# A range check of kept softmax sums, with a general version behind a branch, in a convolution and two-matmul kernel

## The chip, the cores and the metric

The kernel runs on one core of a Trainium2 chip. A core has five engines with instruction streams of their own: TensorE (PE in the profile; PEld is its weight load), VectorE (DVE), ScalarE (ACT), GpSimd (POOL) and SyncE (SP), which here only issues DMA transfers. They meet through semaphores. The metric is device time in microseconds of one execution.

## The reference

```python
def _attn_ref(x, weight_gen):            # x: 8 x 4096 x 192, weight_gen: 8 x 4096 x 8 x 7
    w = weight_gen - np.max(weight_gen, axis=-1, keepdims=True)
    w = np.exp(w)
    w = w / (np.sum(w, axis=-1, keepdims=True) + 1e-09)
    ...                                  # x_unf: the 7 last tokens of x, by head
    out = np.einsum('bshk,bskhg->bshg', w, x_unf)

def _moe_ref(x, w_in, w_out):            # w_in: 192 x 2048, w_out: 2048 x 192
    h = x @ w_in
    g = h - np.tanh(h)
    return g @ w_out
```

Each token has, for each of 8 heads, 7 weights from a softmax. They weigh the token and the 6 before it (a convolution with its own weights at each token). The result, 192 wide, goes through a matmul to 2048, `h - tanh(h)`, and a matmul back to 192. `weight_gen` is drawn from a normal distribution times 0.3, all in float32.

## The kernel before, in words

The 32,768 tokens are cut into 32 blocks of 1024 (`n`, `NTOT` = 32), and a block lies on 128 partitions with 8 tokens each (`J` = 8).

For each block, SP loads `x` and `weight_gen`. ACT takes the exponential without subtracting a maximum (`softmax_exp`). DVE sums over the 7 weights (`softmax_sum`, 64 sums per partition, in a tile `zsum` of which three buffers go round), takes the reciprocal and scales (`softmax_norm`). POOL makes most of the products of weights and tokens, with DMA transfers that add (`dma_sum`), and PE adds what is left while it transposes (`conv_sums`).

The first matmul of block `n` is cut into 16 tiles `f`. Per tile PE fills `ph`, ACT takes the tanh, and DVE subtracts into `gt` (`gemm1`). `ph` comes from three PSUM buffers. Between them PE works at the second matmul of the block before (`out_stream`), whose results ACT copies out (`store_out`), and SP stores a block when its eighth token group is done. A softmax is worked on four blocks ahead of its use: in the loop over `n`, `soft` names that block, and from `n` = 28 on there is none. Where a block has one, DVE does the reciprocal and the scaling between the subtractions of `f` = 14 and `f` = 15.

The order on each engine is written by hand: the whole body stands under `tc.manual_schedule()`, so an engine's instructions come in the order in which the Python code issues them, and semaphores are placed by what each reads and writes.

After the loop, the second matmul of the last block has nothing to lie beside. `gemm2_last(j)` does it by token group `j` (the j-th token of every partition, "token j" for short): 32 matmuls into a bank `po`, a copy of one half by ACT (`ot`), an add by DVE into `out_sb`, and after each second group a store of two of the eight groups on SP. Then the program's end waits for every transfer and the engines meet in a barrier.

Of the kernel before, what the change touches and what calls it, by code (L numbers as in the profile page):

```python
# [8 lines left out]
FP32 = mybir.dt.float32  # L9
BF16 = mybir.dt.bfloat16  # L10

ACT = mybir.ActivationFunctionType
AX = mybir.AxisListType


@with_exitstack
def kernel(
# [20 lines left out]
    JH = J // 2  # L38
    HT = TOK // 2
    NSB = S // TOK  # L40
    NTOT = B * NSB
    NFT = F // P
    NC = D // R
# [7 lines left out]
    HELP = {n: ((n - 2, 3),) for n in (4, 5, 6, 7, 8, 9, 10, 11, 12, 13, 14, 15, 16, 17, 18, 19, 20, 21, 22, 23, 24, 25, 26, 27, 28, 29, 30, 31)} | {9: ((7, 3), (6, 12)), 10: ((8, 3), (7, 12)), 11: ((9, 3), (8, 12)), 12: ((10, 3), (9, 12)), 13: ((11, 3), (10, 12)), 14: ((12, 3), (11, 12))}  # L51
    LAST_TAP = (4, 5, 6, 7, 8)
    X_LATE = ()
    ZERO_AT = 8
    PACE, PACED = None, ()
    SCALE_TWICE = True
# [24 lines left out]
    zero = const.tile([1, D], FP32, name="zero")  # L81
    nc.vector.memzero(zero[:])
    once = const.tile([P, 1], FP32, name="once")

    x_of = {}
    held = {}
# [2 lines left out]
    zsum_of = {}  # L89
    zr_of = {}  # L90
    wsm_of = {}
    prods_of = {}
    to_sum = {}
    conv_of = {}
# [72 lines left out]
    def softmax_exp(n):  # L167
        wg_t = wg_of.pop(n)
        last_exp[0] = nc.scalar.activation(  # L169
            out=wg_t[:].rearrange("p j h k -> p (j h k)"),  # L170
            in_=wg_t[:].rearrange("p j h k -> p (j h k)"),
            func=ACT.Exp,
        )
        e_of[n] = wg_t
# [4 lines left out]
    def softmax_sum(n, j0=0, j1=J):  # L179

        if j0 == 0:
            zsum_of[n] = wgpool.tile([P, J * H], FP32, name="zsum")
        nc.vector.reduce_sum(  # L183
            out=zsum_of[n][:, j0 * H : j1 * H],
            in_=e_of[n][:, j0:j1].rearrange("p j h k -> p (j h) k"),
            axis=AX.X,
        )

    def softmax_recip(n, j0=0, j1=J):
        if j0 == 0:  # L190
# [3 lines left out]
    def softmax_norm(n, bank):  # L194

        wsm = softmax_tile()
        zr_v = bank[:, 512 - J * H : 512]
        nc.vector.reciprocal(zr_v, zsum_of[n][:])  # L198

        def finish():  # L200
            scale(nc.vector, wsm[:], e_of[n], zr_v)

        wsm_of[n] = (wsm, None, None, None)
        return finish

    def softmax_norm_ramp(n, bank):

        softmax_sum(n)
        wsm = softmax_tile()
        zr_v = bank[:, 512 - J * H : 512]  # L210
        nc.vector.reciprocal(zr_v, zsum_of[n][:])  # L211
# [14 lines left out]
        wsm_of[n] = (wsm, wsm_v, None, None)  # L226
# [298 lines left out]
    def out_pairs(m):  # L525
        for _ in range(m):
            next(pairs)

    def gemm2_last(j, f0=0, f1=NFT):

        n = NTOT - 1
        if f0 == 0:
            half[j] = psum_h.tile([P, 2, HT], FP32, name="po2", tag="ph")
        po = half[j]
        col = (j % 2) * HT + (j // 2) * P
        for f in range(f0, f1):
            for r in range(2):
                nc.tensor.matmul(  # L538
                    po[:, r, 0:D],
                    lhsT=g_of[n][f][r * R : (r + 1) * R, col : col + P],  # L540
                    rhs=w_out[r * R : (r + 1) * R, f, :],
                    start=(f == 0),
                    stop=(f == NFT - 1),
                )
# [6 lines left out]
        nc.scalar.activation(out=ot[:], in_=po[:, 0, 0:D], func=ACT.Copy)  # L551
        nc.vector.tensor_add(out_sb[:, j, :], po[:, 1, 0:D], ot[:])
        if j % 2 == 1:
            nc.sync.dma_start(
                out=out[n * TOK : (n + 1) * TOK, :].rearrange("(p j) e -> p j e", p=P)[
                    :, j - 1 : j + 1, :
                ],
                in_=out_sb[:, j - 1 : j + 1, :],
            )

    w_in = const.tile([P, NC, F], BF16, name="w_in")
    w_out = const.tile([P, NFT, D], BF16, name="w_out")

    ctx.enter_context(tc.manual_schedule())

    def load_w_out():
        nc.gpsimd.dma_start(out=w_out[:], in_=moe_w_out.rearrange("(c p) e -> p c e", c=NFT))
# [139 lines left out]
    for n in range(1, NTOT):  # L707
        more = n < NTOT - 1
        finish = []
        plan = FIRST if n == 1 else DOUBLE if n in DOUBLE_IN else APART if n in APART_IN else STEADY  # L710

        soft = [m for m in (n + 3 if n <= AHEAD else n + 4,) if m < NTOT]
        for f in range(NFT):
            ph = gemm1(n, f)
            if n == 1:
                if f == 1:
                    load_wg(5)
                if f == 5:
                    softmax_exp(4)
                steps = ((softmax_sum, 3), (softmax_recip, 3), (softmax_sum, 4))  # L720
                for at, (step, m, h) in zip(plan["sums"], [s + (h,) for s in steps for h in (0, 1)]):
                    if f == at:
                        step(m, h * JH, (h + 1) * JH)
                if f == 5:
                    wsm_of[3] = (softmax_tile(), None, e_of[3], zr_of[3])
                    rest = products(3)
            elif f == 1:
                if soft:
                    softmax_exp(soft[0])
                if n + 2 < NTOT:  # L730
                    rest = products(n + 2)
            if n == AHEAD and f == 4:
                softmax_exp(n + 4)
            if n > 1:
                for h, at in enumerate(plan["sums"]):
                    if soft and f == at:
                        softmax_sum(soft[0], h * JH, (h + 1) * JH)
            if n == AHEAD:
                for at, (step, h) in zip(EXTRA, [(s, h) for s in (softmax_sum, softmax_recip) for h in (0, 1)]):
                    if f == at:  # L740
                        step(n + 4, h * JH, (h + 1) * JH)
                if f == EXTRA[-1]:
                    wsm_of[n + 4] = (softmax_tile(), None, e_of[n + 4], zr_of[n + 4])
            for m in (n + 2, n + 3):
                if (n, f) in HELP.get(m, ()):
                    help(m, ph, J - 1 - HELP[m].index((n, f)))
            if n + 2 < NTOT and f == (9 if n == 1 else max([b for a, b in HELP.get(n + 2, ()) if a == n] + [3])):
                rest()
            if f == (9 if n == 1 else 1) and n > STORE_FIRST:
                loads(n)  # L750
            done = 0
            for chunks, at in sorted((((0, 1), plan["t2"]), ((2,), plan["t1"])), key=lambda c: c[1]):
                if more and at[0] == f:
                    out_pairs(at[1] - done)
# [12 lines left out]
            if f == (9 if n == 1 else 1) and n <= STORE_FIRST:  # L767
                loads(n)

    gemm2_last(0, 0, J)  # L770
    out_pairs(NFT)
    gemm2_last(0, J, NFT)
    for j in range(1, J):
        gemm2_last(j)


# [28 lines left out]
```

## Time and profile before

| | |
|---|---|
| three runs | 745.0, 746.48 (median), 747.21 us |
| span of the profiled execution, first to last instruction | 743.4 us |
| its own device time | not listed; the runs lie 1.6 to 3.8 us above this span |
| mean granted TensorE clock | 0.995 |
| PE / DVE / ACT / POOL busy | 97% / 92% / 86% / 88% of the span |
| last matmul, last add on DVE, last store issued, end of the wait for it | 739.6, 740.3, 740.4, 742.2 us |

The profile is of one execution on the chip. Its page has the busy times of each engine, the span in 40 slices, the DMA queues, the chain of work that ended last, the costliest groups of instructions, and the DMA issues. Groups are named by line of the kernel, engine and operation, "out<-in", with shapes, count, busy time, mean time of one, and what ended the idle time before them. From the trace, questions can be asked of one stretch: busy times in windows, a timeline of an engine, the chain of waits in order of time, or one line's instructions. Matmuls are pipelined, so that a busy PE is not a PE at its peak. SPq is SP's queue: an issue's time there is that of issuing, not of the transfer.

### The profile page before, as it was taken

The numbers are of one execution on the slowest core, as the hardware profiler recorded it, in microseconds if no ns is written. First come the engines' busy times: TensorE is split into PE (matmuls) and PEld (weight loads), VectorE is DVE, ScalarE is ACT, GpSimd is POOL, SyncE is SP. The second block draws the span as 40 slices with busy tenths as digits, with TensorE's granted clock in tenths as the row PEclk, the third lists the DMA queues.
The fourth block names the chain that finished last, engine by engine and source line by source line (L and its number), as shares of the span: only waits on it lengthen the run. The fifth ranks groups of instructions, "written<-read, shape, count | busy, mean of one in ns | idle before, by whom it ended". The sixth has DMA issues, their size and how long they took to land.

```text
span 743.4 us, 30037 instructions
## 1 busy us (share of the span) xinstructions
PE 722.3 (97%) x13616; PEld 556.5 (75%) x13616; DVE 687.4 (92%) x723; ACT 638.8 (86%) x872; POOL 654.5 (88%) x163
## 2 busy tenths in 40 slices
PE   3899999999999999999999999999999999999997
PEld 2477777778777777777777777777777777877777
DVE  7999899999999999999999999999999999988893
ACT  4888888888888888989889999898998989888882
POOL 7999999999999999999999999999999999991000
PEclk9899999999999999999999999999999999999999
DMA  8925367766567668878777977877887877776112
GB/s 236 245 46 161 135 172 185 195 179 149 124 183 184 183 185 224 210 199 203 166 202 209 236 186 204 178 195 205 221 209 195 192 181 194 193 149 110 45 45 86
DMA packets 34269, 130.06 MB, mean 175 GB/s; under 512 B 4591, under 2 KB 9439, under 8 KB 30174
## 3 DMA queue, kind: packets, MB, share of 16 engines
q0 software_dynamic: 19424, 51.12, 40.4%
q1 hardware_dynamic: 14718, 77.03, 27.6%
q8 instruction: 106, 1.74, 0.9%
q14 instruction: 21, 0.17, 0.1%
HBM read 54.52 MB, written 25.17 MB: 107 GB/s over the span
## 4 chain that ended last, share of the span: by engine, by line
PE 92%; DVE 5%; ACT 1%; issue 1%; DMA 1%; SPq 0%; DVEq 0%
PE ph L427 43%; PE obank L495 43%; PE pc L384 4%; DVE gt L441 3%; PE po L538 1%; ACT th L440 1%; DVE pa L299 1%; DMA wg_t<-in_weight_gen_dram 1%; DVE zsum L183 0%; SPq L134 0%; ACT convT L402 0%; DVE obank L211 0%; DVE pa L251 0%; DVE pb L299 0%; SPq L144 0%
## 5 line engine op out<-in xcount | busy, mean ns | idle before, releaser
L441 DVE TENSOR_TENSOR gt<-ph,th 128x1024 bf16<-128x1024 f32 x512 | 601.6, 1217 | 33.4 <-ACT th L440 23.2
L440 ACT ACTIVATE th<-ph 128x1024 f32<-128x1024 f32 x512 | 512.1, 1025 | 69.2 <-PE ph L427 60.3
L427 PE MATMUL ph<-convT,w_in 64*128 64x512 bf16 x3072 | 415.1, 379 | 5.3 <-DVE gt L441 3.3
L495 PEld LDWEIGHTS <-gt 64*128 64x128 bf16 x7936 | 355.6, 94 | 80.6 <-issue 6.3
L495 PE MATMUL obank<-w_out,gt 64*128 64x192 bf16 x7936 | 408.0, 243 | 0.9 <-issue 0.8
L299 POOL TENSOR_TENSOR pa<-x_t,wsm 128x2688 bf16<-128x2688 f32 (+3 forms) x68 | 338.9, 5232 | 0.2
L299 POOL TENSOR_TENSOR pb<-x_t,wsm 128x4608 bf16<-128x4608 f32 (+2 forms) x33 | 283.8, 8601 | 0.7 <-ACT wsm L221 0.5
L427 PEld LDWEIGHTS <-w_in 64*128 64x128 bf16 x3072 | 163.0, 94 | 86.0 <-issue 18.3
L514 ACT ACTIVATE out_sb<-obank 128x192 f32<-128x192 f32 x248 | 81.3, 328 | 11.2 <-PE obank L495 10.3
L410 ACT ACTIVATE convT<-pc 128x1024 bf16<-128x1024 f32 (+1 forms) x62 | 50.1, 810 | 2.9 <-PE pc L384 2.7
L236 POOL DMA_DIRECT2D pa<-pb x28 | 36.0, 1284 | 13.7 <-POOL pb L299 9.1
L384 PEld LDWEIGHTS <-pa 64*128 64x128 bf16 x2064 | 41.5, 100 | 6.8 <-DVE pa L299 1.1
L236 POOL DMA_DIRECT2D pa<-pa x21 | 34.7, 1651 | 9.6 <-DMA pa<-pb 8.9
L384 PE MATMUL pc<-ident,pa 64*128 64x64 bf16 x1968 | 41.2, 191 | 1.8 <-POOL pa L299 0.9
L183 DVE TENSOR_REDUCE zsum<-wg_t 128x32 f32<-128x224 f32 (+1 forms) x61 | 23.6, 387 | 2.9 <-ACT wg_t L169 2.9
L169 ACT ACTIVATE wg_t<-wg_t 128x448 f32<-128x448 f32 x32 | 18.2, 570 | 6.3 <-DMA wg_t<-in_weight_gen_dram 6.2
L251 DVE TENSOR_TENSOR pa<-x_t,ph 128x384 bf16<-128x384 f32 x34 | 18.8, 554 | 2.0 <-DVE ph L250 0.3
L229 DVE TENSOR_TENSOR wsm<-wg_t,pc 128x448 f32<-128x448 f32 x27 | 16.8, 621 | 2.5
L198 DVE RECIPROCAL pc<-zsum 128x64 f32<-128x64 f32 x27 | 14.9, 550 | 0.0
L384 PE MATMUL pc<-ident,pb 64*128 64x64 bf16 x216 | 4.9, 206 | 9.0 <-POOL pb L299 9.0
L384 PEld LDWEIGHTS <-pb 64*128 64x128 bf16 x288 | 6.3, 106 | 9.5 <-POOL pb L299 9.0
L538 PE MATMUL po<-w_out,gt 64*128 64x192 bf16 x256 | 11.2, 243 | 0.0
(27 smaller groups left out, 56.8 us busy)
## 6 DMA issues: line engine op xcount, KB each, us to landing
x_t<-in_x_dram SPq DMA_DIRECT2D x31, 1344.0 KB, 7.9
pa<-pb POOLq DMA_DIRECT2D x28, 1152.0 KB, 9.5
out_dram<-out_sb SPq DMA_DIRECT2D x31, 768.0 KB, 3.9
pa<-pa POOLq DMA_DIRECT2D x21, 768.0 KB, 7.2
wg_t<-in_weight_gen_dram SPq DMA_DIRECT2D x32, 224.0 KB, 7.1
x_t<-in_x_dram SPq DMA_DIRECT2D x1, 768.0 KB
w_out<-in_moe_w_out_dram POOLq DMA_DIRECT2D x1, 768.0 KB, 9.5
out_dram<-out_sb SPq DMA_DIRECT2D x4, 192.0 KB, 3.0
```

What stands on the lines that cost most here:

```text
L183: nc.vector.reduce_sum(out=zsum_of[n][:, j0 * H : j1 * H], in_=e_of[n][:, j0:j1].rearrange("p j h k -> p (j h) k"), axis=AX.X,)
L236: return nc.gpsimd.dma_start(out=out.rearrange("p k j d -> p k (j d)"), in_=in_.rearrange("p k j d -> p k (j d)"), accum_op=mybir.AluOpTyp ...
L251: nc.vector.tensor_mul(pa[:, 0:KH, j, :].rearrange("p k (h g) -> p k h g", h=H), bass.AP(tensor=x_v.tensor, offset=x_v.offset + j * D, ap= ...
L299: return eng.tensor_mul(prod(k0, k1)[:, :, j0:j1].rearrange("p k j (h g) -> p k (j h) g", h=H), bass.AP(tensor=x_v.tensor, offset=x_v.offs ...
L384: nc.tensor.matmul(pc[r][:, col : col + R] if home else pc[:, r, col : col + R], lhsT=prods[c][gi][r * R : (r + 1) * R, 2 * j : 2 * j + 2] ...
L410: last_conv[0] = nc.scalar.activation(out=out, in_=pc[:, :, 0:cols].rearrange("p r (cj t) -> p r cj t", t=R), func=ACT.Copy,)
L427: nc.tensor.matmul(ph[:, r, :], lhsT=w_in[r * R : (r + 1) * R, c, f * P : (f + 1) * P], rhs=convT[r * R : (r + 1) * R, c, :], start=(c == ...
L440: last_act[0] = nc.scalar.activation(out=th[:], in_=ph_f, func=ACT.Tanh)
L441: last_sub[0] = nc.vector.tensor_sub(gt[:], ph_f, th[:])
L495: mm = nc.tensor.matmul(po[:, 0:D], lhsT=g_of[n][f][r * R : (r + 1) * R, col : col + P], rhs=w_out[r * R : (r + 1) * R, f, :], start=(r == ...
L514: last_act[0] = nc.scalar.activation(out=out_sb[:, j, :], in_=po[:, 0:D], func=ACT.Copy)
L538: nc.tensor.matmul(po[:, r, 0:D], lhsT=g_of[n][f][r * R : (r + 1) * R, col : col + P], rhs=w_out[r * R : (r + 1) * R, f, :], start=(f == 0 ...
```

## The change

The kernel leaves the maximum out of its softmax, which is exact as long as the sums stay within the range of float32. The change adds a look at this, and a second version of the whole computation for the case that they don't.

- All sums are kept in one tile, `zall` (128 x 2048, float32), of which block `n` has 64 columns. The three buffers `zsum` go.
- `sums_piece` has eight pieces. 0 to 3 are reductions of 128 x 1024 sums to one column: the maxima of the two halves, then the minima. 4 and 5 compare (`<= 1e30`, `>= 1e-18`), 6 multiplies the answers to two columns and sends them with a DMA on SP to one row of 256, and 7 takes the minimum of that row to an integer, `flag`. Pieces 0, 1 and 2 stand behind tile `f` = 14 of blocks 28, 29 and 30, pieces 3 to 6 behind the last tile of block 31, and 7 ahead of token group 4 of the last block.
- The last block's stores are cut anew: groups 0 and 1, groups 2 and 3, group 4 alone, and groups 5 to 7 together.
- The manual schedule ends, every engine loads `flag` into a register, and a conditional block stands ahead of the last store. If the flag is 0, `general` goes over all 32 blocks again with the maximum subtracted, in loops that run on the chip. If it is 1, which it is for these inputs, nothing of this runs.

In the built program the order on PE, ACT and POOL is as before up to the register load. DVE gets the reductions and comparisons where they are written. SP gets the flag's DMA ahead of the store of block 30, then the stores of groups 0 to 1 and 2 to 3, the register load with a range check of the value, the store of group 4, and the conditional branch. On the way that runs here, SP next waits on each of the eight semaphores of its transfers, so for all that it has issued, jumps over the instructions of the general version (146 on SP), and issues the last store. This store waits for a count of DVE, which DVE raises behind its own register load and branch.

```diff
+    STORES = {1: 0, 3: 2, 4: 4}
+    LAST_STORE = {7: 5}
+    SUM_MAX, SUM_MIN = 1e30, 1e-18
+    CHECK = {(28, 14): (0,), (29, 14): (1,), (30, 14): (2,)}
...
+    zall = const.tile([P, NTOT * J * H], FP32, name="zall")
+    ends = const.tile([P, 4], FP32, name="ends")
+    fine = const.tile([P, 2], FP32, name="fine")
+    fine_row = const.tile([1, 2 * P], FP32, name="fine_row")
+    flag = const.tile([1, 1], mybir.dt.int32, name="flag")
...
-            zsum_of[n] = wgpool.tile([P, J * H], FP32, name="zsum")
+            zsum_of[n] = zall[:, n * J * H : (n + 1) * J * H]
...
+    def sums_piece(i):
+        w = NTOT * J * H // 2
+        if i < 4:
+            op = ALU.max if i < 2 else ALU.min
+            nc.vector.tensor_reduce(ends[:, i : i + 1], zall[:, i % 2 * w : (i % 2 + 1) * w], AX.X, op)
+        elif i == 4:
+            nc.vector.tensor_scalar(ends[:, 0:2], ends[:, 0:2], SUM_MAX, None, op0=ALU.is_le)
+        elif i == 5:
+            nc.vector.tensor_scalar(ends[:, 2:4], ends[:, 2:4], SUM_MIN, None, op0=ALU.is_ge)
+        elif i == 6:
+            nc.vector.tensor_mul(fine[:], ends[:, 0:2], ends[:, 2:4])
+            nc.sync.dma_start(out=fine_row[:], in_=fine[:])
+        else:
+            nc.vector.tensor_reduce(flag[:], fine_row[:], AX.X, ALU.min)
...
+    def store_last(j):
+        n = NTOT - 1
+        j0 = (STORES | LAST_STORE)[j]
+        nc.sync.dma_start(
+            out=out[n * TOK : (n + 1) * TOK, :].rearrange("(p j) e -> p j e", p=P)[:, j0 : j + 1, :],
+            in_=out_of[n][:, j0 : j + 1, :],
+        )
...
-        if j % 2 == 1:
-            nc.sync.dma_start(
...
+        if j in STORES:
+            store_last(j)
...
-    ctx.enter_context(tc.manual_schedule())
+    sched = tc.manual_schedule()
+    sched.__enter__()
...
+            for piece in CHECK.get((n, f), ()):
+                sums_piece(piece)
...
+    for piece in (3, 4, 5, 6):
+        sums_piece(piece)
     gemm2_last(0, 0, J)
     out_pairs(NFT)
     gemm2_last(0, J, NFT)
     for j in range(1, J):
+        if j == 4:
+            sums_piece(7)
         gemm2_last(j)
+    sched.__exit__(None, None, None)
+
+    def general(m, carry):
...
+        nc.vector.tensor_reduce(zr[:], e_v, AX.X, ALU.max)
+        nc.vector.tensor_sub(e_v, e_v, spread(zr[:]))
...
+        with tc.For_i(0, NFT) as f:
...
+        (j,) = LAST_STORE
+        last = slice(LAST_STORE[j], j + 1)
+        nc.vector.tensor_copy(out_of[NTOT - 1][:, last, :], out_sb[:, last, :])
+
+    good = nc.values_load(flag[:], min_val=0, max_val=1)
+    with tc.If(good < 1, preferred_fallthrough_block=False):
+        with tc.For_i(0, B) as b:
+            carry = xpool.tile([P, HALO + J, D], FP32, name="x_t")
+            nc.vector.memset(carry[0:1, 0:HALO, :], 0.0)
+            with tc.For_i(0, NSB) as s:
+                general(b * NSB + s, carry)
+    store_last(J - 1)
```

More of the change, by code (lines that the diff above doesn't have):

```diff
@@ L13 @@
 AX = mybir.AxisListType
+ALU = mybir.AluOpType
 @with_exitstack
@@ L197, in softmax_norm @@
         zr_v = bank[:, 512 - J * H : 512]
-        nc.vector.reciprocal(zr_v, zsum_of[n][:])
+        nc.vector.reciprocal(zr_v, zsum_of[n])
         def finish():
@@ L210, in softmax_norm_ramp @@
         zr_v = bank[:, 512 - J * H : 512]
-        nc.vector.reciprocal(zr_v, zsum_of[n][:])
+        nc.vector.reciprocal(zr_v, zsum_of[n])
         if n == 2:
@@ L552, in gemm2_last @@
         nc.vector.tensor_add(out_sb[:, j, :], po[:, 1, 0:D], ot[:])
-        if j % 2 == 1:
[L554 to L559, printed above, removed]
+        if j in STORES:
+            store_last(j)
     w_in = const.tile([P, NC, F], BF16, name="w_in")
     w_out = const.tile([P, NFT, D], BF16, name="w_out")
-    ctx.enter_context(tc.manual_schedule())
+    sched = tc.manual_schedule()
+    sched.__enter__()
     def load_w_out():
@@ L773, with rows, spread @@
     for j in range(1, J):
+        if j == 4:
+            sums_piece(7)
         gemm2_last(j)
+    sched.__exit__(None, None, None)
+    def general(m, carry):
+        x_t = xpool.tile([P, HALO + J, D], FP32, name="x_t")
+        def rows(p0, p1, r0, r1):
+            first = x.rearrange("b s d -> (b s) d")[bass.ds(m * TOK, 1)]
+            nc.sync.dma_start(
+                out=x_t[p0:p1, r0:r1, :],
+                in_=bass.AP(
+                    tensor=first.tensor,
+                    offset=first.offset + (p0 * J - HALO + r0) * D,
+                    ap=[[J * D, p1 - p0], [D, r1 - r0], [1, D]],
+                ),
+            )
+        rows(0, P, HALO, HALO + J)
+        rows(1, P, 0, HALO)
+        nc.sync.dma_start(out=x_t[0:1, 0:HALO, :], in_=carry[0:1, 0:HALO, :])
+        nc.sync.dma_start(out=carry[0:1, 0:HALO, :], in_=x_t[P - 1 : P, J : J + HALO, :])
+        e_t = wgpool.tile([P, J, H, K], FP32, name="wg_t")
+        nc.sync.dma_start(
+            out=e_t[:],
+            in_=weight_gen.rearrange("b s h k -> (b s) h k")[bass.ds(m * TOK, TOK)].rearrange(
+                "(p j) h k -> p j h k", p=P
+            ),
+        )
+        e_v = e_t[:].rearrange("p j h k -> p (j h) k")
+        zr = wgpool.tile([P, J * H], FP32, name="zr")
+        def spread(v):
+            return v.rearrange("p (n o) -> p n o", o=1).to_broadcast([P, J * H, K])
+        nc.vector.tensor_reduce(zr[:], e_v, AX.X, ALU.max)
+        nc.vector.tensor_sub(e_v, e_v, spread(zr[:]))
+        nc.scalar.activation(
+            out=e_t[:].rearrange("p j h k -> p (j h k)"),
+            in_=e_t[:].rearrange("p j h k -> p (j h k)"),
+            func=ACT.Exp,
+        )
+        nc.vector.reduce_sum(out=zr[:], in_=e_v, axis=AX.X)
+        nc.vector.reciprocal(zr[:], zr[:])
+        nc.vector.tensor_mul(e_v, e_v, spread(zr[:]))
+        total = papool.tile([P, J, D], FP32, name="total", tag="pa")
+        part = papool.tile([P, J, D], FP32, name="part", tag="pa")
+        summed = pbpool.tile([P, J, D], BF16, name="pb")
+        x_v = x_t[:]
+        for k in range(K):
+            to = total if k == 0 else part
+            nc.vector.tensor_mul(
+                to[:].rearrange("p j (h g) -> p (j h) g", h=H),
+                bass.AP(tensor=x_v.tensor, offset=x_v.offset + k * D, ap=[x_v.ap[0], [G, J * H], [1, G]]),
+                e_t[:].rearrange("p j h (k o) -> p k (j h) o", o=1)[:, k].to_broadcast([P, J * H, G]),
+            )
+            if k > 0:
+                nc.vector.tensor_add((summed if k == K - 1 else total)[:], total[:], part[:])
+        prods_of[NTOT] = [[summed[:]]] * NC
+        conv(NTOT, (0, 1), (2,))
+        convT = conv_of.pop(NTOT)
+        out_sb = opool.tile([P, J, D], FP32, name="out_sb")
+        nc.vector.memset(out_sb[:], 0.0)
+        with tc.For_i(0, NFT) as f:
+            w_f = tpool.tile([P, NC, P], BF16, name="w_f", tag="th")
+            nc.sync.dma_start(out=w_f[:], in_=w_in[:, :, bass.ds(f * P, P)])
+            w_o = tpool.tile([P, D], BF16, name="w_o", tag="th")
+            nc.sync.dma_start(out=w_o[:], in_=w_out[:, bass.ds(f, 1), :].rearrange("p o e -> p (o e)"))
+            ph = psum_h.tile([P, 2, HT], FP32, name="ph", tag="ph")
+            for c in range(NC):
+                for r in range(2):
+                    nc.tensor.matmul(
+                        ph[:, r, :],
+                        lhsT=w_f[r * R : (r + 1) * R, c, :],
+                        rhs=convT[r * R : (r + 1) * R, c, :],
+                        start=(c == 0),
+                        stop=(c == NC - 1),
+                    )
+            th = tpool.tile([P, TOK], FP32, name="th")
+            gt = gpool.tile([P, TOK], BF16, name="gt0", tag="gt0")
+            ph_f = ph[:].rearrange("p r t -> p (r t)")
+            nc.scalar.activation(out=th[:], in_=ph_f, func=ACT.Tanh)
+            nc.vector.tensor_sub(gt[:], ph_f, th[:])
+            for j in range(J):
+                po = psum_h.tile([P, 2, HT], FP32, name="po2", tag="ph")
+                col = (j % 2) * HT + (j // 2) * P
+                for r in range(2):
+                    nc.tensor.matmul(
+                        po[:, r, 0:D],
+                        lhsT=gt[r * R : (r + 1) * R, col : col + P],
+                        rhs=w_o[r * R : (r + 1) * R, :],
+                        start=True,
+                        stop=True,
+                    )
+                for r in range(2):
+                    nc.vector.tensor_add(out_sb[:, j, :], out_sb[:, j, :], po[:, r, 0:D])
+        nc.sync.dma_start(
+            out=out[bass.ds(m * TOK, TOK), :].rearrange("(p j) e -> p j e", p=P),
+            in_=out_sb[:],
+        )
+        (j,) = LAST_STORE
+        last = slice(LAST_STORE[j], j + 1)
+        nc.vector.tensor_copy(out_of[NTOT - 1][:, last, :], out_sb[:, last, :])
```

## The prediction

> **What bounds the kernel now.** First the page's head, engine lines and code queues:
>
> ```profile
> span 743.4 us, 30037 instructions
> ...
> PE 722.3 (97%) x13616; PEld 556.5 (75%) x13616; DVE 687.4 (92%) x723; ACT 638.8 (86%) x872; POOL 654.5 (88%) x163
> ...
> q8 instruction: 106, 1.74, 0.9%
> q14 instruction: 21, 0.17, 0.1%
> ```
>
> PE is the bound up to the end of its work. The two instruction queues bring code while the program runs: q8 1.74 MB for PE's 27,232 records, 64 bytes each, so q14's blocks of 0.17 MB / 21 = 8.1 KB hold about 127 instructions of the other engines. That matters for a jump.
>
> Second, the chain of waits in the last 20 us, the sync queue (SP) in order of time, and the end's own line on SP:
>
> ```profile
> 729.67 9.91 PE po L538 x237
> 739.59 0.02 issue
> 739.61 0.34 ACT ot L551
> 739.95 0.02 issue
> 739.97 0.36 DVE out_sb L552
> ```
>
> ```profile
> 740.36 0.33 SPq L554 DMA_DIRECT2D out_dram<-out_sb  x1
> ```
>
> ```profile
> L800 SPq EVENT_SEMAPHORE  x5: 17/28/28, 742.2 to 743.3; - x5
> ```
>
> The last add ends at 740.33, the last store is issued at 740.36, SP's wait for it ends at 742.2 (1.87 us after issue), and 1.2 us of closing barrier follow. Nothing computes after 740.33: whatever delays the last store, or makes it longer, lengthens the run one for one.
>
> Third, busy times in five stretches cut where blocks n = 26 to 30 start their subtractions (PE, PEld, DVE, ACT, POOL, then clock and DMA):
>
> ```profile
> 598.43:620.52 22.09, 22.03 (x406) 16.79 (x402) 21.07 (x23) 19.80 (x27) 21.79 (x6) 1.00 0.80 193
> 620.52:642.51 21.99, 21.99 (x407) 16.92 (x403) 21.08 (x22) 19.75 (x27) 21.67 (x6) 1.00 0.80 193
> 642.51:664.35 21.84, 21.84 (x405) 17.52 (x402) 19.49 (x18) 19.35 (x26) 21.30 (x6) 1.00 0.61 127
> 664.35:686.22 21.87, 21.87 (x406) 17.14 (x402) 19.50 (x19) 19.38 (x26) 8.38 (x3) 1.00 0.69 142
> 686.22:708.03 21.81, 21.81 (x406) 16.88 (x402) 18.94 (x16) 19.32 (x26) 0.00 (x0) 1.00 0.13 44
> ```
>
> From block 28 on DVE has no softmax left: 1.58 us less work, and the block becomes 0.19 us shorter (22.04 to 21.85). So DVE work costs about 0.12 us per us here.
>
> **The change, part by part.** Prices are from this one execution. Its span is 743.4 us; its own device time isn't listed. The median of the runs, 746.48, lies 3.1 us above the span (the runs: 1.6 to 3.8), and I add the sum to it. A difference under 0.3% (2.24 us) is about what a measurement of this kernel can't tell from no change.
>
> Keeping all sums in one tile changes names alone: order and waits of every engine are as before up to the first added instruction. Cost nothing, and nothing had to hide it.
>
> *Three reductions in the loop* (f = 14 of n = 28, 29, 30). The rows for a sum over the same type are
>
> ```profile
> L183 DVE TENSOR_REDUCE zsum<-wg_t 128x32 f32<-128x224 f32 x58 | 21.8, 375 | 0.0
> ...
> L183 DVE TENSOR_REDUCE zsum<-wg_t 128x64 f32<-128x448 f32 x3 | 1.8, 614 | 2.9 <-ACT wg_t L169 2.9
> ```
>
> so 239 ns per 224 elements and 614 + 576 x 1.07 = 1.23 us for 1024. Between gt14 and gt15 blocks 26 and 27 hold a reciprocal and a scaling, 0.55 + 0.62 us, which these blocks don't; the reduction takes their place. At 0.12 per us: 3 x 1.23 x 0.12 = +0.43 us. Ends: 0, and 3.7 if each pushes PE one for one. Behind the reduction wait gt15 and then PE, for its ph buffer.
>
> *The rest of the check on DVE*, after the last gt (ends 728.49): 1.23 us and three instructions on 2 columns, by the smallest row of the kind (a 128x16 copy, 190 ns) 0.57, ready at about 730.3. DVE sat idle until 730.73, so nothing on the path; without that cover it would push adds that each have 0.96 us idle before them.
>
> *The flag's transfer* goes out on SP at 730.3, ahead of the last full-block store (730.07 before, ready data). That store moves to about 731.1 (an SP issue took 0.33 to 0.97); with the usual 3.9 us it lands by 735, 8 us before the end. The flag's reduction (256 elements, 0.41) stands on DVE between the adds of tokens 3 and 4, at 735.05 to 735.46, and add 4 began at 736.01: hidden if the transfer lands in 4.7 us. A store took 1.9 to 3.9, a weight_gen load under load 7.1.
>
> *The start of the last store.* It waits for two chains.
>
> DVE: after its last add it loads the flag into a register, branches, and only then raises the count that the store waits for. No row shows a register load. From below it is a sequencer's instruction (28 ns) under the 0.36 us add, cost 0; from above a whole DMA, 1.87. It reads one word and returns, so I take the last store's round trip without issue (0.33) and movement (0.8, four slices of the strip below): 0.75. From 739.99 that ends at 740.75, 740.8 with branch and count, which is +0.45.
>
> SP: flag known at 735.46, register load to 736.2, a range check, then the store of token 4, whose add ended at 736.37: issued 736.40 as its pair store would allow. Then comes the new wait: ahead of the jump SP waits for all eight DMA semaphores, so for the landing of token 4: 738.27 at 1.87 us, 739.4 at the 3.0 us that the 735.08 store took. Behind it on SP stands only the last store. Then the jump, about 738.4. On SP it skips 146 instructions of the general version, more than a block of 127, so its target isn't in the block that runs, and at best just asked for. What a fetch costs: lower end a resident target, 28 ns; next an idle transfer, 1.87; upper end what SP itself shows:
>
> ```profile
> 262.34 0.97 SPq L120 DMA_DIRECT2D wg_t<-in_weight_gen_dram  x1
> 269.80 0.34 SPq L518 DMA_DIRECT2D out_dram<-out_sb  x1
> ```
>
> SP was through its last issue at 263.3; the code block I ascribe to it (81 of its 209 instructions are behind it, and the next such block comes after the end, 128 on) moved at 267.1, 3.7 us later at the least. The DMA was busy then and is nearly idle at 738, but it is the only fetch of this engine's code in the run, so I take 3.7: start at 742.1, +1.74. With token 4 landing at 739.4 it is +2.85; with a fetch under 2.4 us DVE's +0.45 decides.
>
> [...]
>
> *The last store's size*: 288 KB for 192. The DMA strip from 736 to 744, 0.2 us a slice:
>
> ```profile
> GB/s 353 346 85 8 8 15 15 15 0 0 0 0 54 361 376 192 0 0 0 0 0 0 0 0 0 31 323 376 254 0 0 0 0 0 0 0 0 0 41 0
> ```
>
> The last store is the four slices 31 to 254; 96 KB at 376 GB/s are +0.26 us. If a code block shares one of its DMA engines, it takes 3.0 for 1.87, as the 735.08 store did: up to +1.1 more.
>
> Closing waits and barrier stay: the added waits are met long before, and the other engines reach the barrier under the store. SP's four register moves at the start lie beside POOL's barrier, which released at 0.66.
>
> **Sum:** 0.43 + 1.74 + 0.26 = +2.43 us, 748.9.
>
> **Rivals.**
> 1. *Not slower: the jump's code is there in time.* Any fetch under 2.4 us. For: the DMA is idle at 738, and a whole store takes 1.87. Against: the 3.7 above. 0.43 + 0.45 + 0.26 = +1.1: 747.6.
> 2. *DVE becomes the bound in the three blocks.* For: 92% busy; idle before gt15 and the next gt0 is 0.40 + 0.66, under 1.23. Against: blocks 26 and 27 with 1.17 us in that place are only 0.19 longer. 3.7 for 0.43: 752.2.
> 3. *A late flag.* The transfer writes 128 pieces of 8 bytes; at the 7.1 us of a loaded DMA it lands at 737.4, add 4 and all after it move by 2.0 us. Decides from a landing past 735.6. 750.9.
> 4. *Nothing is seen, or a gain*: jump, load and reductions all hidden: 746.5 to 746.7. Only other tile addresses would speak for a gain.
>
> **How the numbers follow.** Mine 0.55 (own range 747.8 to 750.3; 0.42 slower by over 0.3%, 0.13 within), rival 1 0.31 (0.28 within, 0.03 slower), rival 2 0.07 and rival 3 0.04 (slower), rival 4 0.03 (0.02 faster). Faster 0.02, same 0.42, slower 0.56. The range 747.0 to 751.0 holds mine with a late token 4, and rival 1; left out are rivals 2 and 4 and the far ends.
>
> **What would show it.** The last store on SP at 742.1, an SP gap of about 3.7 us ahead of it with one q14 block inside, and DVE done by 740.8: mine. The store right after DVE's branch at 740.8: rival 1. The reductions at 1.23 us and blocks 28 to 30 at about 22.0 us, not 23: against rival 2. The add of token 4 at 736.0: against rival 3. I am wrong if the register load is far from 0.75 us, if the fetch starts earlier than the jump, or if the flag reaches SP so late that token 4's store is issued after 736.4.

## The result, and the profile after

The changed kernel takes 747.71 us (median of 11 runs, 746.64 to 748.71); the kernel before, run beside it, 745.95 us (11 runs, 744.72 to 747.21). The ratio is 1.0024, 95% interval 1.0015 to 1.0032: 1.8 us slower (1.1 to 2.4), which is clear of noise and in its middle within the 0.3% bound. 748.9 was predicted. The profiled execution took 747.28 us, 1.8 above its span.

The head of the changed kernel's page, with its code queues:

```profile
span 745.5 us, 30082 instructions
...
PE 722.3 (97%) x13616; PEld 556.7 (75%) x13616; DVE 692.6 (93%) x731; ACT 639.1 (86%) x872; POOL 654.6 (88%) x163
...
q8 instruction: 107, 1.75, 0.9%
q14 instruction: 25, 0.20, 0.1%
```

DVE has 5.2 us more to do in 8 more instructions, PE not 0.1 us. Five more blocks of code moved, one for PE (q8) and four for the other engines (q14); the span is 2.1 us longer.

The chain of waits of the last 16 us, in order of time (start, us, what):

```profile
730.49 9.91 PE po L572 x237
740.40 0.02 issue
740.43 0.34 ACT ot L585
740.77 0.02 issue
740.79 0.36 DVE out_sb L586
```

From the last matmuls to the last add it is the same chain as before, to 0.01 us, 0.82 us later. So the change acts in two places: ahead of this chain, and behind the last add. Behind it, first the instructions of single lines (queue, operation, number: duration in ns, minimum, median and maximum; first and last start):

```profile
L917 SPq TENSOR_LOAD <-flag x1: 525/525/525, 736.3 to 736.3; - x1
L917 DVEq TENSOR_LOAD <-flag x1: 538/538/538, 740.8 to 740.8; - x1
...
L918 SPq COMPARE_BRANCH  x2: 46/48/49, 737.9 to 739.4; - x2
...
L558 SPq EVENT_SEMAPHORE  x4: 17/17/28, 732.8 to 740.8; - x4
L558 SPq DMA_DIRECT2D out_dram<-out_sb x4: 332/336/577, 733.3 to 741.6; - x4
```

Then the waits of SP in the last 10 us (us in total, times, longest):

```profile
SPq L950 <- DMA out_dram<-out_sb: 1.7, 1, 1.7
...
SPq L918 <- SPq L918: 0.9, 2, 0.6
SPq L558 <- DVEq L918: 0.7, 1, 0.7
```

SP takes its jump at 739.35 and is back with its next instruction (a wait on landings of long ago) at 740.83, 1.48 us later. It then waits 0.7 us more, for DVE at line 918, the branch. DVE's register load starts behind the issue of its last add, at 740.81, takes 0.54, and its count goes up at 741.52. The last store is issued at 741.57. So DVE's register load sets the store, and SP's jump is hidden by 0.7 us.

The transfers from 738 to 745 us, 0.175 us a slice (share of the DMA engines in tenths, then GB/s):

```profile
DMA  0196000100000000000130010599951200000000
GB/s 18 44 325 211 0 0 0 47 0 0 0 0 0 0 0 0 0 0 0 47 94 0 0 47 0 237 395 395 355 185 66 86 13 0 0 0 0 0 0 0
```

The lone 47s and the 94 are blocks of code. The first began to move at 739.25, 0.10 us ahead of SP's jump. The next three begin to move 0.65, 0.80 (16 KB, PE's) and 1.36 us behind the last add's start, where the store's issue is at 0.78, and a last one of 8 KB at 2.68, within the slice of 86. The store is the stretch from 237 on, and it has a tail, 66 86 13, that the store of before hadn't. Thirteen of the store's sixteen parts have landed 2.06 us after issue, the last three only by 2.63.

It helps to cut the end at fixed points, read from the trace, in us: A, start of the last add to issue of the last store; B, issue to the end of SP's wait for it; C, from there to the end of the span.

| | A | B | C | end |
|---|---|---|---|---|
| before | 0.38 | 1.87 | 1.17 | 3.42 |
| changed | 0.78 | 2.65 | 1.30 | 4.73 |

The end costs 1.31 us: 0.40 in A, 0.78 in B, 0.13 in C.

Ahead of the chain, busy times in the blocks n = 28, 29 and 30 of the changed kernel, cut as before (stretch, its length, then PE, PEld, DVE, ACT, POOL, clock, DMA):

```profile
643.07:665.17 22.10, 22.10 (x406) 17.63 (x402) 20.54 (x20) 19.39 (x27) 21.62 (x6) 1.00 0.61 129
665.17:687.04 21.87, 21.87 (x405) 17.15 (x402) 20.54 (x20) 19.39 (x26) 8.12 (x3) 1.00 0.68 143
687.04:708.86 21.82, 21.82 (x406) 16.87 (x402) 19.99 (x18) 19.34 (x27) 0.00 (x0) 1.00 0.10 40
```

DVE has 1.05 us more in each. Blocks 29 and 30 are as long as before to 0.01 us; block 28 is 0.26 us longer. Up to block 28 executions differ from one another by up to 1.9 us (it starts at 642.51 before, 643.07 here, 642.2 to 644.1 in the runs below), with no order by kernel, so a single profile says nothing there.

So the theory after the profile: 0.40 us by DVE's register load, 0.23 to 0.26 by the store's size, 0.5 by code that moves beside the store, 0.13 in closing, 0.26 in block 28. The rivals: SP's jump decides after all; the store is long by its size alone; the reductions cost what was predicted.

### The profile page after: what moved, and what is told of

It is laid out like the page before. It is cut to its first block, busy times and chain, and to the rows that moved or that the text cites. A ratio compares the mean times of both kernels' runs of the same rounds, so it can differ in the third digit from the quotient of the medians.

```text
span 745.5 us, 30082 instructions
## 1 busy us (share of the span) xinstructions
PE 722.3 (97%) x13616; PEld 556.7 (75%) x13616; DVE 692.6 (93%) x731; ACT 639.1 (86%) x872; POOL 654.6 (88%) x163
## 4 chain that ended last, share of the span: by engine, by line
PE 91%; DVE 6%; issue 1%; ACT 1%; DMA 0%; DVEq 0%
PE obank L521 43%; PE ph L453 43%; PE pc L410 4%; DVE gt L467 4%; PE po L572 1%; DVE pa L325 1%; ACT th L466 1%; DVE pb L325 0%; DVE zall L193 0%; DMA wg_t<-in_weight_gen_dram 0%; DVE obank L237 0%; DVE obank L255 0%; ACT wg_t L179 0%; DVE pa L277 0%; ACT convT L428 0%
## 5 line engine op out<-in xcount | busy, mean ns | idle before, releaser
L193 DVE TENSOR_REDUCE zall<-wg_t 128x32 f32<-128x224 f32 (+1 forms) x61 | 23.7, 388 | 2.9 <-ACT wg_t L179 2.9
L224 DVE RECIPROCAL pc<-zall 128x64 f32<-128x64 f32 x27 | 14.9, 551 | 0.0
```

Source lines behind the costliest of these rows:

```text
L193: nc.vector.reduce_sum(out=zsum_of[n][:, j0 * H : j1 * H], in_=e_of[n][:, j0:j1].rearrange("p j h k -> p (j h) k"), axis=AX.X,)
```

## The experiments

Edits are against the changed kernel where nothing else is said. A, B, C and the end are as above, in us.

**The stores' new cut alone**, on the kernel before:

```diff
-        if j % 2 == 1:
+        if j in (1, 3, 4, 7):
+            j0 = {1: 0, 3: 2, 4: 4, 7: 5}[j]
...
```

> The kernel before with its last stores cut as in the changed one (tokens 0-1, 2-3, 4, 5-7), without check or branch. Three lengths are read at the end: A, from the start of the last add to the issue of the last store (before 0.39, changed 0.78 us); B, from that issue to the end of SP's wait for it (1.87, 2.65); C, the closing barrier (1.17, 1.28). Theory (the register load lengthens A, code blocks fetched during the store lengthen B, the jump is hidden): A 0.39, B 2.1 (96 KB more at 376 GB/s), C 1.17: +0.26 us, no measurable difference. Rival 'size' (a store of three tokens takes 2.65 whatever else runs): B 2.65, +0.8 us.

Measured: A 0.38, B 2.10, C 1.17, end 3.65; 1.0005 (0.9996 to 1.0014). The size alone is +0.23. The store's other 0.55 us in the changed kernel is not its size.

**The branch with next to nothing in it**: the general version is left out, and a memset stands in its place, which doesn't run.

```diff
     with tc.If(good < 1, preferred_fallthrough_block=False):
-        with tc.For_i(0, B) as b:
-            ...
+        nc.vector.memset(out_of[NTOT - 1][:, 5:J, :], 0.0)
```

> The changed kernel without the general version: the conditional block holds one small memset, so that SP has nothing to jump over, no eight waits, and no code to fetch; this leaves the general version's computation out. Theory: A stays near 0.75 (DVE still loads its register behind the last add), B falls from 2.65 to about 2.1, C as it is: 0.5 to 0.6 us less than the changed kernel. Rival 'jump' (SP's jump sets the start of the last store): A falls to 0.45. Rival 'size': B stays at 2.65.

Measured: A 0.78, B 2.07, C 1.00, end 3.85; 1.0010 (1.0000 to 1.0019). SP's jump takes 0.19 us here, for 1.48, and A is the same: in this kernel the jump isn't what the store waits for, the register load is. B loses its 0.6 us, and no block of code moves beside the store. The transfers from 739.38 us on, 0.15 us a slice (the lone 55 is the next block, which begins when the store has landed):

```profile
GB/s 246 10 0 0 0 0 0 0 0 0 0 0 0 0 0 0 0 0 0 0 0 0 92 338 430 445 353 307 0 0 0 55 0 0 0 0 0 0 0 0
```

C was expected as it is and is 0.30 us shorter, for which no run shows a reason.

**The register loads ahead of the last token group**, which puts SP's behind the store of token 4:

```diff
+        if j == 7:
+            good = nc.values_load(flag[:], min_val=0, max_val=1)
         gemm2_last(j)
...
-    good = nc.values_load(flag[:], min_val=0, max_val=1)
```

> The changed kernel with the register load of every engine ahead of the last token group, so that on DVE it lies in the idle time before the last add. Theory: A falls from 0.78 to about 0.45 (the add's 0.36, a branch and a count); B stays near 2.65; 0.3 us less. Rival 'jump': A stays at 0.78, since SP comes back from its jump no earlier. If PE's own load stalls it, the last adds come later than 1.32 us after one another.

Measured: A 1.68, B 2.50, end 5.48; 1.0033 (1.0021 to 1.0045). A miss. SP's load now ran in line behind that store; its jump came 0.5 us ahead of the last add's start, it was back 2.09 us later, and the store left 0.09 behind that. So SP's chain has 0.7 us of slack in the changed kernel, and a later jump decides.

**A jump that must come late**: stores of tokens 4 and 5 together, and a last store of two.

```diff
-    STORES = {1: 0, 3: 2, 4: 4}
-    LAST_STORE = {7: 5}
+    STORES = {1: 0, 3: 2, 5: 4}
+    LAST_STORE = {7: 6}
```

> The changed kernel with stores of tokens 0-1, 2-3, 4-5 and a last store of 6-7. Theory: the store of 4-5 is issued 1.3 us later than that of token 4 and lands 0.4 us before the last add's start; its wait, the jump and 1.4 us for code then end about 1.4 us after the last add's start: A 1.4 instead of 0.78, B about 0.26 less; 0.3 to 0.4 us slower than the changed kernel. Rival 'no fetch' (SP sat 1.4 us behind its jump for another reason, such as DVE): A stays at 0.78 and the kernel is 0.26 us faster.

Measured: A 1.45, B 2.59, end 5.35; 1.0036 (1.0022 to 1.0050). SP's jump starts at -0.16 from the last add's start and SP is back at +1.36: the stall is real, 1.52 us, and when it can't hide it is paid. And B is 2.59, where about 2.4 was expected, for a store of 192 KB, which takes 1.87 in the kernel before: 13 parts have landed at 1.83, the last at 2.58. Size is not what makes it long.

**The last store delayed past the code**, by five lines like this one:

```diff
+    nc.vector.tensor_copy(out_of[NTOT - 1][:, 5:J, :], out_of[NTOT - 1][:, 5:J, :])
     store_last(J - 1)
```

> The changed kernel with five extra copies in place of the last three tokens (128x576 each) on DVE behind its branch, ahead of the last store. The copies change no value; they only delay the last store by about 2 to 2.5 us, so that it is issued when the blocks of code fetched at the end (0.65 to 1.4 us behind the last add's start) have moved. Measured from the last add's start: issue of the last store at about 3 us in place of 0.78. Theory (code blocks moving beside the store make its last pieces late): from issue to the end of SP's wait 2.07 to 2.2 us in place of 2.65, as in the version without a general version (2.07). If a further block moves then, as one did at 2.68 us in the changed kernel, up to 2.4. Rival (the long landing comes from something fixed in the changed program, not from the code blocks): 2.65 again.

The store is issued at 744.60, 3.85 us behind the last add's start (3 expected; one time, 749.83), and B is 2.07. The program's transfers from 742.31 us on, 0.15 us a slice:

```profile
DMA  0010000000000000000018998800000000000000
GB/s 0 0 55 0 0 0 0 0 0 0 0 0 0 0 0 0 0 0 0 0 77 338 415 461 353 307 16 0 0 0 0 0 0 0 0 0 0 0 0 0
```

The same program with the same branch and the same store: with the code out of the way (the 55 is the last block) the tail is gone. This shows that the late parts come from the code blocks. Which DMA engine a block shares with the store the trace doesn't say; three of sixteen parts being late fits a few shared engines. A store that all fourteen kernels have shows the same on a small scale. It leaves 4.9 us ahead of the last add's start (at 735.08 in the kernel before), and beside it one block of PE's code begins to move, 0.29 to 0.86 us behind its issue. In every profile fifteen of its parts have landed by 1.83 to 1.88 us and the sixteenth only by 2.75 to 3.36: one block, one late part. Of the last four stores of each profile, those without a block beside them have at most one part that is late against the others, by up to 0.5 us.

**The preferred way turned round**:

```diff
-    with tc.If(good < 1, preferred_fallthrough_block=False):
+    with tc.If(good < 1, preferred_fallthrough_block=True):
```

> The conditional block with its preferred way turned round: SP takes its jump ahead of the eight waits and not behind them, but DVE has to take a jump too before it raises the count that the last store waits for. Theory: SP's jump starts at about 0.6 us behind token 4's store issue and is back after its fetch (1.4 to 2.1 us), still ahead of the last add; the waits on landed stores follow and cost 0.05 to 0.2 each. The store then goes by DVE: register load 0.54 and a taken jump 0.5 if its target is at hand: from the last add's start to the store's issue 1.2 us (0.78 in the changed kernel); if DVE's jump needs a fetch, 2.2 us or more. Rival (jumps cost nothing here): 0.8 us. Issue to end of wait 2.5 to 2.65 us by the theory of the code blocks.

Measured: A 1.25, B 2.59, C 1.29, end 5.14 (one time, 747.65). SP jumps at 737.52 and is back 2.55 us later, still 0.6 ahead of the last add; the eight waits cost 0.06 to 0.09 each. The store then waits for DVE, whose jump stands ahead of its count: 0.47 us over the changed kernel, where DVE loses 0.56 by a jump of its own behind the store's issue. As expected.

**The register load off DVE's end**:

```diff
-        if j == 4:
+        if j == 2:
             sums_piece(7)
+        if j == 4:
+            good = nc.values_load(flag[:], min_val=0, max_val=1)
...
-    good = nc.values_load(flag[:], min_val=0, max_val=1)
```

> The flag's reduction is moved from ahead of token group 4 to ahead of token group 2, and the register loads of all engines from behind the last group to ahead of group 4; the branch stays ahead of the last store. Theory: DVE's 0.54 us register load no longer stands behind the last add, only its branch (0.05 to 0.1 us). SP's order is as in the changed kernel, its jump is back at about the same time, 0.04 us behind the last add's start, so the store can be issued 0.45 to 0.5 us behind the last add's start in place of 0.78. Issue to end of wait as in the changed kernel, 2.65 us (between 2.07 and 2.65 if the code blocks fall otherwise). Timed: 0.3 us under the changed kernel's 1.0024, so 1.0020, with an interval that touches it. Rival (the time behind the last add is set by SP's jump): 0.78 again or more.

Measured: A 0.44, B 3.16, C 1.30, end 4.90; 1.0024 (1.0013 to 1.0035). A does what was expected: DVE's load is 0.34 us of the end. But the store then runs into the same blocks of code. Three of the four keep their place against its issue to 0.1 us; PE's keeps its place against the last add (0.78 us) and so begins 0.34 us behind the issue, for 0.02. The last part lands 1.1 us behind the thirteenth, and nothing is won. That PE's block makes the difference is not shown; this is one profile. The transfers from 739.5 us on, 0.15 us a slice:

```profile
GB/s 55 0 0 0 0 0 0 0 0 0 0 0 0 0 55 0 0 109 0 55 92 399 338 384 384 185 31 101 31 15 31 15 15 0 0 0 0 0 0 0
```

**The branch behind all stores**:

```diff
-    STORES = {1: 0, 3: 2, 4: 4}
-    LAST_STORE = {7: 5}
+    STORES = {1: 0, 3: 2, 5: 4}
+    LAST_STORE = {7: 6}
...
+    store_last(J - 1)
     sched.__exit__(None, None, None)
...
-    store_last(J - 1)
```

> The changed kernel with the branch behind all stores of the last block, which are cut as before (two token groups each); the general version would come after them. Theory: the last store is issued 0.38 us behind the last add's start, as before, and nothing fetches code beside it: 1.87 us to the end of its wait. Then SP waits for all landings, jumps (1.4 to 2.1 us until its next instruction) and closes: tail 0.38 + 1.87 + 0.5 for the waits + 1.5 to 2.1 + 1.3 = 5.5 to 6.1 us, against 4.73 in the changed kernel: 0.8 to 1.4 us slower than it, 1.0035 to 1.0043. Rival (jumps on this path are as cheap as with code at hand, 0.4 us): 4.5 us, no slower than the changed kernel.

Measured: A 0.39, B 3.47, C 2.60, end 6.45; 1.0048 (1.0034 to 1.0062). Slower than the changed kernel, as expected, but by another way: I had written that nothing fetches code beside this store. The other engines take their jumps there, four blocks of code (one of them PE's) begin to move within it, 0.41 to 1.89 us behind its issue, and its last part lands at 3.46 us where thirteen have at 1.82. SP's jump then takes only 0.51 us. SP's instructions at the branch and at the end:

```profile
L919 SPq EVENT_SEMAPHORE  x8: 17/17/17, 741.5 to 744.6; - x8
L919 SPq COMPARE_BRANCH  x2: 46/48/49, 741.4 to 744.7; - x2
...
L950 SPq EVENT_SEMAPHORE  x14: 17/28/28, 745.2 to 747.1; - x14
```

**No reductions in the loop**:

```diff
-    CHECK = {(28, 14): (0,), (29, 14): (1,), (30, 14): (2,)}
+    CHECK = {(1, 14): ()}
...
+    nc.vector.tensor_copy(ends[:, 0:3], zall[:, 0:3])
     for piece in (3, 4, 5, 6):
```

> The changed kernel without the three reductions of 128x1024 in blocks 28, 29 and 30; three sums are copied to their places instead, so the check then covers only the last reduction. The end of the program is as in the changed kernel. The prediction's term: 0.43 us less, 1.0018 in place of 1.0024. Theory after the profile (the blocks 28 to 30 were no longer relative to before than the block ahead of the first reduction): 0 to 0.1 us less, 1.0023 to 1.0024. Rival (the rest of the slowdown, some 0.5 us of 1.8 that the tail doesn't explain, is all from the reductions): 0.5 us less, 1.0017. Start of the last subtraction in the profile: 727.3 to 728.1, with 0.8 us of difference between executions, so that the timed ratio decides.

Measured: 1.0016 (1.0000 to 1.0032), too wide to tell. The profile tells: blocks 28, 29 and 30 take 22.11, 21.86 and 21.81 us, as with the reductions (22.10, 21.87, 21.82). So in the profile they cost nothing, and the 0.26 us of block 28 isn't theirs.

**Each reduction twice**:

```diff
             for piece in CHECK.get((n, f), ()):
                 sums_piece(piece)
+                sums_piece(piece)
```

> The changed kernel with each of the three reductions in blocks 28, 29 and 30 done twice (the second repeats the first), 2.46 us of DVE work in a block in place of 1.23. The tail is as in the changed kernel. Theory (hidden behind PE with room to spare): blocks 28, 29 and 30 take 22.1, 21.87 and 21.81 us as they do with one reduction each, 0 added. The prediction's rate of 0.12 us per us: 0.15 more in each block, 0.44 us in all. Rival (DVE's idle time ahead of the next subtractions, 0.40 and 0.66 us, is all the room there is): 2.46 less 1.06, 1.4 us more in each of the blocks, up to 4 us in all.

Measured: 1.0071 (1.0057 to 1.0085). The three blocks:

```profile
642.23:665.48 23.25, 22.90 (x419) 18.20 (x414) 21.67 (x20) 20.41 (x27) 22.71 (x6) 1.00 0.63 132
665.48:688.36 22.88, 22.16 (x400) 16.75 (x400) 21.66 (x21) 19.55 (x26) 6.97 (x3) 1.00 0.60 129
688.36:711.24 22.88, 22.16 (x400) 16.75 (x400) 21.01 (x19) 19.55 (x26) 0.00 (x0) 1.00 0.09 37
```

1.15, 1.01 and 1.06 us more, and PE is no longer busy throughout. My theory of room to spare and the prediction's rate of 0.12 both fall; the rival (1.4 each) has the manner right. DVE's timeline around the reduction of block 28 shows it (start, us; in brackets the idle time before). Before:

```profile
660.85 1.22 DVE L441 TENSOR_TENSOR gt<-ph,th 128x1024 bf16<-128x1024 f32 x1 [0.69 <-ACT th L440]
662.47 1.23 DVE L441 TENSOR_TENSOR gt<-ph,th 128x1024 bf16<-128x1024 f32 x1 [0.40 <-ACT th L440]
664.35 2.36 DVE L441 TENSOR_TENSOR gt<-ph,th 128x1024 bf16<-128x1024 f32 x2 [0.66 <-PE ph L427]
```

Changed:

```profile
661.66 1.23 DVE L467 TENSOR_TENSOR gt<-ph,th 128x1024 bf16<-128x1024 f32 x1 [0.95 <-ACT th L466]
662.80 1.21 DVE L204 TENSOR_REDUCE ends<-zall 128x1 f32<-128x1024 f32 x1
663.92 3.60 DVE L467 TENSOR_TENSOR gt<-ph,th 128x1024 bf16<-128x1024 f32 x3
```

Doubled:

```profile
661.97 2.46 DVE L204 TENSOR_REDUCE ends<-zall 128x1 f32<-128x1024 f32 x2
664.35 5.74 DVE L467 TENSOR_TENSOR gt<-ph,th 128x1024 bf16<-128x1024 f32 x5
```

One reduction fills the idle 0.40 and 0.66 us, and the next subtractions follow without a gap; it fits almost exactly. The second finds no room and is paid nearly in full.

**The branch without the check** and **the check without the branch**. In the first there are no reductions, the sums keep their three buffers, and the flag is set to 1:

```diff
-            zsum_of[n] = zall[:, n * J * H : (n + 1) * J * H]
+            zsum_of[n] = wgpool.tile([P, J * H], FP32, name="zsum")
...
-            sums_piece(7)
+            nc.vector.memset(flag[:], 1)
```

> The branch without the check: the sums stay in three buffers, there are no reductions and no flag transfer; DVE sets the flag to the constant 1 at the place of its reduction, and register loads, branch, general version and stores are as in the changed kernel. What it settles is the 0.27 us by which block 28 (from the first subtraction of its block to that of the next) is longer in all profiles with the branch (22.08 to 22.17) than in those without (21.82 and 21.84), with or without the three reductions. Theory 1 (the branch's added instructions shift PE's blocks of code, whose fetch in block 28 moves from 14.33 to 14.6 us behind the block's start): 22.1 here. Theory 2 (the place of the sums in memory): 21.83. The tail as in the changed kernel in both: 0.78 us from the last add's start to the store's issue, 2.6 to 2.8 us from there to the end of its wait. Timed: 0.4 us for the register load, 0.78 for the store, 0.1 closing, and 0.27 by theory 1: 1.0018 to 1.0022; 1.0017 by theory 2.

In the second `general`, the register loads and the conditional block are deleted:

```diff
-    good = nc.values_load(flag[:], min_val=0, max_val=1)
-    with tc.If(good < 1, preferred_fallthrough_block=False):
-        ...
     store_last(J - 1)
```

> The check without the branch: sums in one tile, all reductions, the flag's transfer and its last reduction as in the changed kernel, but no engine loads the flag and there is no branch and no general version. Block 28 by theory 1 of the run with the branch alone: 21.83 us; by theory 2: 22.1. The tail as in the kernel before with stores cut anew: 0.38 us from the last add's start to the store's issue, 2.1 from there to the end of its wait, 3.65 in all (3.42 before). Timed: 0.23 us, 1.0003; 1.0007 by theory 2; the prediction's term for the reductions (0.43) would give 1.0009.

Block 28 with the branch alone:

```profile
643.87:665.69 21.82, 21.82 (x405) 17.46 (x401) 19.49 (x18) 19.34 (x26) 21.00 (x6) 1.00 0.60 125
```

and with the check alone:

```profile
642.95:665.07 22.12, 22.12 (x406) 17.63 (x403) 20.53 (x20) 19.38 (x27) 21.59 (x6) 1.00 0.61 129
```

The branch's part in theory 1 falls: the 0.26 us goes with the check's tiles and not with the branch. All nine other runs with one reduction in a block or none, and with these tiles, have block 28 at 22.08 to 22.27; the three kernels without them have 21.82 to 21.84. In the trace it is one pause of PE between two matmuls into `ph`, 16.6 us behind the block's start, for which the trace names no wait. Ahead of it the trace shows one difference, and it keeps the other part of theory 1 open. A block of PE's code begins to move 14.33 to 14.40 us behind the start of block 28 in the three kernels without the tiles and 14.57 to 14.62 in the eleven with them, and in these eleven PE goes on 2.29 to 2.46 us behind that (in the three it passes the same place 2.2 to 2.3 us behind it, without a pause). A wait for this block fits as well as the place of a tile in memory; neither was tried, and the cause is open.

The ends: with the check alone A 0.38, B 2.07, C 1.43, 3.88 in all; 1.0024 (1.0006 to 1.0042), where the profile's parts give 0.7 us, 1.0010. With the branch alone A 1.28, B 3.19, C 1.36, 5.83 in all; 1.0041 (1.0020 to 1.0061). Its tail was expected to be the changed kernel's and isn't: SP jumped 0.88 us ahead of the last add's start, was back 2.07 us later, and decided.

**Do the parts add up?** The end, and blocks 28 to 31 up to the last subtraction, each less the kernel before (3.42 and 84.76 us), against the timed ratio times 746 us:

| | end | blocks 28 to 31 | sum | timed |
|---|---|---|---|---|
| changed | +1.31 | +0.25 | 1.6 | 1.8 (1.1 to 2.4) |
| new cut alone | +0.23 | -0.02 | 0.2 | 0.4 (-0.3 to 1.0) |
| empty branch | +0.43 | +0.24 | 0.7 | 0.7 (0 to 1.4) |
| load behind token 4 | +2.06 | +0.27 | 2.3 | 2.5 (1.6 to 3.4) |
| last store of two | +1.93 | +0.28 | 2.2 | 2.7 (1.6 to 3.7) |
| load off DVE's end | +1.48 | +0.26 | 1.7 | 1.8 (1.0 to 2.6) |
| no loop reductions | +1.45 | +0.26 | 1.7 | 1.2 (0 to 2.4) |
| reductions twice | +1.38 | +3.41 | 4.8 | 5.3 (4.3 to 6.3) |
| branch behind stores | +3.03 | +0.43 | 3.5 | 3.6 (2.5 to 4.6) |
| branch alone | +2.41 | -0.01 | 2.4 | 3.1 (1.5 to 4.6) |
| check alone | +0.46 | +0.27 | 0.7 | 1.8 (0.4 to 3.1) |

Every sum lies in its interval, but the intervals are wide: by the times alone the check without the branch (1.0024) costs as much as the whole change, and only the profiles tell the two apart. The sums are of one profile each and mostly up to 0.7 us under the timed middle (1.1 for the check alone); what that rest is isn't settled.

## Why the prediction was right and wrong

The range held the time (747.0 to 751.0), and the direction is right, but the likeliest case, slower by over 0.3% at 0.56, isn't the one that came: within 0.3% had 0.42. The step that was taken to be deciding failed. The sum was +2.43 us; 1.6 to 1.8 were measured. Of the 1.2 us between 748.9 and 747.71, 0.5 is the base: the median of before was 746.48 in three runs and 745.95 in eleven. That the sum came as near as it did is in part luck: start of the store, reductions and size were put 1.8 us too high together, and three terms that the sum had at nothing (code beside the store 0.55, block 28 0.26, closing 0.13) gave 0.9 of it back.

- *The sums in one tile, at nothing*: wrong as far as known, +0.26 us in block 28, which came with the check's tiles or with something that came with them. I argued from order and waits, and these are indeed as before. What else can change with them, the place of tiles or the timing of code, I had excluded without a row.
- *Three reductions, +0.43 at 0.12 us per us*: 1.21 us each as predicted (1.23), cost 0. The rate was a slope between blocks with a softmax and without, applied to work that fits into idle time. The doubled run shows a step in place of a slope: nothing while DVE's 1.06 us of idle time and a little more lasts, then 1.0 to 1.15 us for 1.21. Rival 2's threshold was the right form; its size missed by the last 0.1 us that made it fit.
- *Rest of the check and the flag's transfer, hidden*: right. The flag's reduction ran at 735.79 and took 0.40 us; the wait ahead of the add of token 4 was still for ACT.
- *The last store's start, SP's side*: right up to the jump. Against the last add's start, token 4's store was put at -3.57 us and came at -3.55, its landing at -1.70 and -1.70, the jump at -1.57 and -1.44. Then the failing step: a fetch of 3.7 us was taken, 1.48 was measured, and in the other runs that jump over the general version ahead of the last store 0.95 to 2.55. My 3.7 came from a block ascribed to SP in the middle of the run, with the DMA engines busy. Counted from the same instruction of SP (its 81st), that block began 1.2 to 4.1 us later in the fourteen profiles, 2.4 in the changed kernel's own: it was one value out of a spread and no price. And at the end the block came 0.10 us ahead of the jump, which I had named as a sign of being wrong. The bound that I gave, a fetch under 2.4 us leaves the decision to DVE, was right, and 1.48 is under it. With it rival 1 describes what happened.
- *DVE's side, +0.45*: measured +0.40 (the register load took 0.54 us for 0.75, but branch and count took 0.2 for 0.05).
- *The store's size, +0.26*: 0.23 by the run with the cut alone. The term that I left at its end of the range, a code block beside the store (up to +1.1), is the largest that there is: B grew by 0.78, of which 0.55 is code.
- *Closing the same*: +0.13.

Rival 1 with the measured terms is thus 0.26 + 0.40 + 0.78 + 0.13 = 1.6 for its 1.1.

That a jump past the block that runs has to wait for its code was my estimate, from the size of q14's blocks, and the runs agree with it in kind: SP's next instruction came 0.19 us behind the jump with next to nothing to skip, and 0.95 to 2.55 us behind it with the general version to skip ahead of the last store. The jump's own row, a compare-and-branch, shows 46 ns in the changed kernel, and that is not what the engine loses; what SP waits for in that time the runs don't show.

## What to carry to other kernels

Here the branch at the end cost nothing by SP's jump, which was hidden, 0.40 us by a register load and 0.55 by what its code did to the last transfer; where the jump came later it was paid as well (A of 1.45 us in the run with a last store of two, 0.78 in the changed kernel). So find out when the blocks of code move, and look at the last parts of the store that leaves beside them. Where several chains end at one store, a chain with 0.7 us of slack is hidden in one build and decides in the next; moving a load off one of them moved the wait (0.34 us won at issue, 0.51 lost in landing). Work that went into idle time here had a step and not a slope (nothing for the first 1.21 us, 1.0 to 1.15 for the second), and one run with that work doubled showed how near the step is.

## What the runs showed of the hardware that was not expected

- A register load of one word from on-chip memory took 0.46 to 0.55 us on every engine at the quiet end, and 0.85 and 1.01 us (PE, POOL) in the run that issued them at 734.4 and 734.5 us.
- Skipping the same general version cost SP 0.95 to 2.55 us, by the run; a block of code moved between 0.8 us ahead of the jump and 1.0 behind it, and the trace doesn't say whose it was. But in all nine of these builds SP was back 1.56 to 1.78 us after this block began to move, wherever the jump lay, so the stall looks like what is left of a wait for the block; that is argued from the times and not tried.
- Blocks of 8 and 16 KB made a store of 192 or 288 KB finish 0.4 to 1.6 us later, though the strip shows DMA engines free: most parts landed on time (thirteen of sixteen by 1.82 to 2.06 us in most of these runs, 2.40 in the run with the branch alone).
- PE paused 0.26 us (0.24 to 0.43 by the run) at one place of block 28 with the check's tiles and without them not, and the trace names nothing that it waited for.
